# Seven half-block products in place of eight for the folded weight of an mLSTM and feed-forward kernel

## The chip, the cores and the metric

The kernel runs on one core of a Trainium2 chip. A core has TensorE (matrix products, results go to PSUM), VectorE and ScalarE (both read PSUM), GpSimd (works on SBUF alone) and queues that issue DMAs. PSUM has eight banks here; four belong to one pool of this kernel and are handed out again and again. The metric is the device time of one execution in microseconds (us).

## The reference, cut to what matters

An mLSTM cell over 768 tokens, for 4 batches of 8 heads of 40, gives `y`; its rows, 3072 tokens of 320, go through a multiplicative feed-forward block. There is no nonlinearity after the product of the two branches:

```python
x = attn_out.transpose(0, 2, 1, 3).reshape(B * S, H * D)   # 3072 x 320
a = x @ w1                                                # 320 x 1024
b = x @ w2                                                # 320 x 1024
h = a * b @ w3                                            # (a * b) @ w3, 1024 x 1024
out = h @ w_out                                           # 1024 x 320
```

So `w3` and `w_out` can be multiplied once: `w3o = w3 @ w_out`, 1024 x 320, the folded weight; then `out = (a * b) @ w3o`.

## The kernel before, in words

All of it is written out by a loop over `s`, called a step in this document. A step handles one block of 128 tokens of one batch in the cell (there are 24), and beside it a share of the feed-forward work of earlier blocks. The order of TensorE's instructions is the order in which they are written (`mm` and `transpose` chain each to the one before, L84 to L95); the other engines keep their own order too, in-order queues each, and an instruction waits there for what it reads and for the buffer that it writes.

In the steps that matter here, 9 to 16, TensorE does this, in order: the transposes of a finished block of `y` (`px`, L485); the products of the folded weight (`fold`, L253); two blocks of the feed-forward's first layer (`up`, tiles `pa`, `pb`, `pa`, `pb`, with their remainders `wr` in `up_rest`); and the cell's products (tiles `cell`). Every `px`, `wp`, `pa` and `pb` takes one bank of the pool of four (`mps`, L77). Their readers free them: `px` and `pa` are read by ScalarE, `pb` by VectorE (L639), `wp` by ScalarE (L264).

VectorE does in a step, in order: the two products L639 that finish the first layer's blocks; the cell's outputs and states, L423 to L445 (here `h` at L423 is the first that reads the step's own `cell` products); the transposes of the next `k` and `q` (L317); and two chunks of `w3` turned from their packed form to float32 and transposed (`convert`: L199, L200, L248). Sixteen such chunks, of half a row block each, are turned: one in step 7, three in step 8, two in each of steps 9 to 14 (`n_cvt`, L814).

GpSimd decays the states (L335: one decay that waits for nothing new, one that waits for VectorE's L404), weights `v` (L330), masks the weights of the next block (L308), and copies the last columns of `y` (L476), which the `px` transposes of the following step but one read.

The folded weight takes eight rounds, one for each 128 rows of `w3`: eight products of 128x128 by 128x320 each, summed in one bank, then one scaled copy by ScalarE:

```python
        for ki in range(FO):
            mm(wp, w3T[:, ki, :], wo[:, ki, :], start=(ki == 0), stop=(ki == FO - 1))
        nc.scalar.mul(out=w3o[:, ko, :], in_=wp, mul=UP ** -2)
```

A product in float32 appears in the trace as two matmul records, so the 64 products are 128 records. A row block's round runs in the step after the next one that follows its conversion: two in step 10, one in each of steps 11 to 16. In step 16 the second layer begins (`ffn_out`, tiles `po`), which reads `w3o`.

Of the kernel before, what the change touches and what calls it, by code (L numbers as in the profile page):

```python
# [8 lines left out]
FP = mybir.dt.float32  # L9
U32 = mybir.dt.uint32  # L10
AF = mybir.ActivationFunctionType
OP = mybir.AluOpType
UP = 2.0 ** 9
# [3 lines left out]
def kernel(  # L17
# [26 lines left out]
    nc = tc.nc  # L44
# [3 lines left out]
    P = 128  # L48
# [6 lines left out]
    DM = H * D  # L55
    BH = B * H
    DFF = moe_w1.shape[1]
    FO = DFF // P
# [6 lines left out]
    const = ctx.enter_context(tc.tile_pool(name="const", bufs=1))  # L65
    wst = ctx.enter_context(tc.tile_pool(name="wst", bufs=2))
# [10 lines left out]
    def mps(shape, name):  # L77
        pool = banks.pop(0)
        banks.append(pool)
        return pool.tile(shape, FP, name=name, tag="m")  # L80
# [3 lines left out]
    def in_order(ins):  # L84

        if last:
            tc.add_manual_dep(ins.ins, last.pop().name, mybir.DependencyInfo(
                mybir.DependencyClass.NoSync, mybir.DependencyReason.DATA), reason="in_order")
        last.append(ins.ins)

    def mm(out, lhsT, rhs, start=True, stop=True):
        in_order(nc.tensor.matmul(out, lhsT=lhsT, rhs=rhs, start=start, stop=stop))  # L92
# [75 lines left out]
    wo = const.tile([128, FO, DM], FP, name="wo")  # L168
# [3 lines left out]
    w3o = const.tile([128, FO, DM], FP, name="w3o")  # L172
    CW = 512
# [23 lines left out]
    def to_f32(dst, raw):  # L197
        bits, V = dst.bitcast(U32), nc.vector
        V.tensor_scalar(out=bits, in0=raw[:, :, 1], scalar1=3, scalar2=None, op0=OP.logical_shift_left)  # L199
        V.tensor_tensor(out=bits, in0=bits, in1=raw[:, :, 0], op=OP.add)  # L200
# [8 lines left out]
    pend, scaled = [], []  # L209
# [18 lines left out]


    w3T_t = {}  # L230
    turned_w3, ready_w3 = [], []

    def scale_next(early=False):
        scaled.append(pend.pop(0))
        scale(scaled[-1][1], early)

    def convert():
        if not scaled:
            scale_next()
        dst, raw, ko, half = scaled.pop(0)  # L240
        if dst is not None:
            to_f32(dst, raw)
            return
        w3 = wst.tile([128, CW], FP, name="w3", tag="w3")
        to_f32(w3, raw)
        if half == 0:
            w3T_t[ko] = wst.tile([128, FO, 128], FP, name="w3T", tag="w3T")
        nc.vector.transpose(out=w3T_t[ko].rearrange("c k (m r) -> c m k r", r=32)[:, 2 * half:2 * half + 2],  # L248
                            in_=w3.rearrange("r (m c k) -> r m k c", m=2, k=FO))
        if half:  # L250
            turned_w3.append(ko)

    def fold():  # L253
        while ready_w3:
            w3_mm(ready_w3.pop(0))
        ready_w3.extend(turned_w3)
        turned_w3.clear()

    def w3_mm(ko):
        w3T = w3T_t.pop(ko)  # L260
        wp = mps([128, DM], "wp")
        for ki in range(FO):
            mm(wp, w3T[:, ki, :], wo[:, ki, :], start=(ki == 0), stop=(ki == FO - 1))
        nc.scalar.mul(out=w3o[:, ko, :], in_=wp, mul=UP ** -2)  # L264


    qT_t, kT_t, vw_t, before_t, y_t, x_t = {}, {}, {}, {}, {}, {}
# [25 lines left out]
    def rows_of_u(n):  # L293
        c, b = divmod(n, B)
        nc.vector.transpose(out=weights_tile(n).rearrange("p h (t i) -> p h t i", t=2),
                            in_=UT[:, :, (0, 2, 1)[c], b * H:(b + 1) * H].rearrange("p t h -> p h t").unsqueeze(3).to_broadcast([P, H, 2, 32]))
# [171 lines left out]
    def x_turn(n):  # L468
        gr, j = divmod(n, GT)
        if j == 0:  # L470
            x_t[gr] = ffn.tile([128, KC, TG], FP, name="xT", tag="xT")
        nc.vector.transpose(out=x_t[gr][:, :, j * P:(j + 1) * P].rearrange("c k (m r) -> c k m r", r=32),
                            in_=back_t.pop(n).rearrange("r m k c -> r k m c"))
# [21 lines left out]
    f_sb, a, F, U, on = (gates[0:RG, i * TC:(i + 1) * TC] for i in range(5))  # L495
# [72 lines left out]
    for i, r in enumerate(third):  # L568
        V.tensor_tensor_scan(out=M[r, 1:GC + 1], data0=F3[r, :, L - 1], data1=U3[r, :, L - 1], initial=M[r, 0:1],
                             op0=OP.add, op1=OP.max)  # L570
# [24 lines left out]
    for i, r in enumerate(third):  # L595
        nc.gpsimd.tensor_tensor(out=pick[r, :, i, :], in0=pair[r].to_broadcast([BH, B * NP, GC]), op=OP.mult,
                        in1=dec[r].unsqueeze(1).to_broadcast([BH, B * NP, GC]))
# [11 lines left out]
    nc.scalar.activation(out=g, in_=U, func=AF.Exp)  # L609
    scale_next(True)  # L610
    convert()

    ffn = ctx.enter_context(tc.tile_pool(name="ffn", bufs=2))


    ab_t = {}
# [51 lines left out]
    def up_by_seven(gr, f, bank, aside_by):  # L668
# [61 lines left out]

        return single, shared, left, product

    def ffn_out(blocks, pos=None):

        pos = pos or [mps([P, DM], "po") for _ in blocks]
        for (gr, j), po in zip(blocks, pos):
            for f in range(FO):
                mm(po, ab_t[gr][j // 2][:, f, j % 2 * P:(j % 2 + 1) * P], w3o[:, f, :], start=(f == 0), stop=(f == FO - 1))
        for (gr, j), po in zip(blocks, pos):
            o_sb = ffn.tile([P, DM], FP, name="o_sb", tag="o_sb", bufs=2)  # L740
            nc.scalar.copy(out=o_sb, in_=po)  # L741
            t0 = j * S + gr * P
            nc.scalar.dma_start(out=out[t0:t0 + P, :], in_=o_sb)


    KH, NH = FO // 2, DM // 2

    def out_weight_sums():

        T_o.extend(m[:, i * KH * NH:(i + 1) * KH * NH].rearrange("p (f n) -> p f n", n=NH)  # L750
                   for m, i in ((v_all, 0), (gates, 0), (gates, 1), (q_all, 0)))
        (B11, B12), (B21, B22) = ([w3o[:, k * KH:(k + 1) * KH, i * NH:(i + 1) * NH] for i in range(2)] for k in range(2))
        T1, T2, T3, T4 = T_o
        for dst, p, q in ((T1, B12, B11), (T2, B22, T1), (T3, B22, B12), (T4, B21, T2)):
            yield nc.gpsimd.tensor_tensor(out=dst, in0=p, in1=q, op=OP.subtract)

    T_o, S_o = [], {}
    wsums = out_weight_sums()

    def quarters_of_ab(gr, j):  # L760
        return [[ab_t[gr][j][:, k * KH:(k + 1) * KH, t * P:(t + 1) * P] for k in range(2)] for t in range(2)]
# [1 line left out]
    def ab_sums(gr, j):  # L763
        mem = [t.rearrange("p h d -> p (h d)") if j == 0 else io.tile([P, H, L], FP, name="pw", tag="pw", bufs=5)
               .rearrange("p h t -> p (h t)") for t in kbuf]
        S1, S2, S3, S4 = S_o[gr, j] = [t.rearrange("p (f t) -> p f t", t=P) for t in mem]
        (A11, A12), (A21, A22) = quarters_of_ab(gr, j)
        for dst, p, q, op in ((S1, A21, A22, OP.add), (S2, S1, A11, OP.subtract), (S3, A11, A21, OP.subtract),
                              (S4, A12, S2, OP.subtract)):
            nc.vector.tensor_tensor(out=dst, in0=p, in1=q, op=op)  # L770

    def out_by_seven(gr, j, sums=None):
# [25 lines left out]
        for t in range(2):  # L798
# [3 lines left out]
    ups = [(gr, [f, f + 1], slice(j * 2 * P, (j + 1) * 2 * P)) for gr in range(3) for j in range(2)  # L802
           for f in range(0, FO, 2)]
    downs = [(gr, j) for gr in range(NG) for j in range(GT)][:14]
    outs = [(gr, j) for gr in range(3, NG) for j in range(2)][1:]
    summed = list(outs)
    sevens = [(gr, f) for gr in range(3, NG) for f in range(FH)]
# [5 lines left out]
    todo = w12[5:] + [("wo", i, 0) for i in range(FO)] + [("w3", ko, part) for ko in range(FO) for part in range(2)]  # L813
# [6 lines left out]
    for s in range(len(n_up)):  # L820
# [28 lines left out]
        while s >= N_DVE and turned < min(s - 2, NY):  # L849
            x_trans(turned)  # L850
            turned += 1
        fold()
        if s >= len(n_up) - 2:
            ab_sums(*summed.pop(0))
        def pairs():
# [62 lines left out]
        with tc.issue_after(gated.ins) if gated else nullcontext():  # L918
            if seven:
                seven[3]()  # L920
            for _ in range({NU: 1, NU + 1: 3}.get(s, 0)):
                next(wsums)
            if s == NU + 1:
                ab_sums(*summed.pop(0))
            if NY <= s - 2 < NU:
                x_turn(s - 2)
            for n in () if s == 1 else (s + 2,) if s < B else (s + 2, s + 3) if s == B else (s + 3,):
                if n < N_U:
                    rows_of_u(n)
            if N_DVE <= s + 1 < NU:  # L930
                gated = turn(s + 1)
            if s - 2 in range(4 * GT - 1, NU, GT):
                token_sums((s - 2) // GT)
            if s < len(n_up) - 2 and n_out[s + 1] and s > NU + 2:
                ab_sums(*summed.pop(0))
# [31 lines left out]
        with tc.issue_after(gated.ins) if N_DVE <= s + 1 < NU else nullcontext():  # L967
            for _ in range(n_cvt[s] if s < len(n_cvt) else 0):
                convert()
                converted += 1  # L970
        if s >= ahead:
            while pend and len(scaled) < 2:
                scale_next()
# [6 lines left out]
            for ins in keep_order(front):  # L980
                behind.enter_context(tc.issue_after(ins))
    behind.close()
    assert not ups and not sevens and not downs and not outs and not summed and not todo and not pend and not turned_w3 and not ready_w3, (len(ups), len(downs), len(todo), len(pend))
# [1 line left out]
_INS = ['q', 'k', 'v', 'i_gate', 'f_gate', 'o_gate', 'moe_w1', 'moe_w2', 'moe_w3', 'moe_w_out']  # L985
_OUTS = [((3072, 320), 'float32')]
# [25 lines left out]
```

## Time and profile before

| what | value |
|---|---|
| median of 3 runs | 426.35 us (425.69 to 426.39) |
| the profiled execution | 427.89 us, of which the program's span is 425.8 us |
| TensorE busy | 414.1 us, 97% |
| VectorE, ScalarE, GpSimd busy | 313.5, 150.1, 154.3 us |
| products of the folded weight (`wp`) | 128 records, 35.9 us, between 108.3 and 209.7 us |
| steps 9, 10, 11, 12, 13, 14, 15 by the start of `px` (step 9: of `pa`) | 96.6, 107.2, 127.7, 142.9, 158.9, 174.2, 189.5 us |

A busy share says how long an engine had something in it, not what sets the end. The profile's groups give counts and durations by line and tile; the timeline gives the order on one engine, with the idle time before an instruction and what ended it; the answer by windows gives busy time, the TensorE clock that was granted and DMA traffic in chosen stretches.

### The profile page before, as it was taken

Reading aid. Unit: us, or ns where it says so; the run is one execution under the profiler, and the core shown is the slowest. Engines: PE = TensorE matmul, PEld = TensorE weight load, DVE = VectorE, ACT = ScalarE, POOL = GpSimd, SP = SyncE. Lnnn points to the kernel's source line nnn. Section 1 sums busy time; section 2 is a strip of 40 time slices with the busy share of each in tenths; the row PEclk is TensorE's granted clock in tenths of the full one; section 3 lists DMA queues with packets and bytes.
Section 4 is the critical chain, followed back from the end, with each engine's and each line's share of the span. In section 5 each row is a group of like instructions: output and inputs, shape, how many; then the busy total and the mean of one; then the engine's idle time right before and its main releaser. Section 6 shows DMA issues by size and latency. Waiting matters only on the chain.

```text
span 425.8 us, 13079 instructions
## 1 busy us (share of the span) xinstructions
PE 414.1 (97%) x5353; PEld 335.3 (79%) x5353; DVE 313.5 (74%) x635; ACT 150.1 (35%) x404; POOL 154.3 (36%) x211
## 2 busy tenths in 40 slices
PE   7989989999999999999999999999999999999996
PEld 4768878888688788787777778788778879888896
DVE  6676986888949779778736966596868699575971
ACT  4766865567723623630433313032311110210000
POOL 4421342233303303303307751546453587542100
PEclk9989999999999999999999999999999999999999
DMA  8999998598977776985425675756421120000001
GB/s 186 204 173 245 214 144 140 134 193 180 215 183 154 166 182 135 181 164 105 89 80 130 153 141 121 142 133 117 87 44 36 35 39 2 31 2 31 2 32 62
DMA packets 135211, 51.15 MB, mean 120 GB/s; under 512 B 109360, under 2 KB 126960, under 8 KB 135152
## 3 DMA queue, kind: packets, MB, share of 16 engines
q1 hardware_dynamic: 131552, 46.29, 53.9%
q10 hardware_dynamic: 3600, 4.03, 2.7%
q8 instruction: 42, 0.69, 0.7%
q14 instruction: 17, 0.14, 0.1%
HBM read 44.50 MB, written 5.80 MB: 118 GB/s over the span
## 4 chain that ended last, share of the span: by engine, by line
PE 53%; issue 20%; DVE 7%; POOL 7%; SPq 7%; DMA 5%; ACT 1%; POOLq 0%; DVEq 0%
PE cell L92 17%; PE pa L92 12%; PE o L92 8%; PE pb L92 8%; PE p L92 3%; POOL pw L308 3%; SPq L184 3%; DVE w3T L666 2%; PE pt L95 1%; POOL vw L330 1%; SPq L148 1%; DMA raw<-in_moe_w_dram 1%; PE fill L92 1%; POOL raw L659 1%; POOL state L335 1%
## 5 line engine op out<-in xcount | busy, mean ns | idle before, releaser
L335 POOL TENSOR_TENSOR state<-state,decay 128x164 f32<-128x164 f32 x40 | 20.0, 500 | 154.8 <-DVE state L404 129.0
L92 PE MATMUL pa<-xT,w 128*128 128x256 f32 x240 | 60.4, 382 | 0.0
L92 PEld LDWEIGHTS pa<-xT,w 128*128 128x128 f32 x240 | 44.4, 190 | 6.8 <-DVE h L430 0.4
L303 ACT ACTIVATE pw<-pw,aT 128x64 f32<-128x64 f32 x184 | 46.4, 339 | 3.2 <-ACT o_sb L741 1.9
L92 PE MATMUL pb<-xT,w 128*128 128x256 f32 x192 | 45.4, 379 | 0.0
L729 POOL TENSOR_TENSOR ab<-ab,a_sb 128x512 f32<-128x512 f32 x22 | 29.4, 1356 | 32.2 <-DVE ab L684 32.2
L92 PEld LDWEIGHTS pb<-xT,w 128*128 128x128 f32 x192 | 36.4, 190 | 5.0
L711 POOL TENSOR_TENSOR wo<-wo 128x512 f32<-128x512 f32 x22 | 27.4, 1268 | 29.8 <-DVE wo L686 29.8
L92 PE MATMUL pa<-xT,wr 64*64 64x256 f32 x384 | 37.0, 386 | 0.5 <-DVE wr L200 0.5
L92 PE MATMUL wp<-wo,w3T 128*128 128x320 f32 x128 | 35.9, 433 | 1.1 <-DVE ab L639 0.6
L308 POOL TENSOR_SCALAR_AFFINE_SELECT pw<-pw 64x512 f32<-64x512 f32 x48 | 35.8, 746 | 3.0 <-ACT pw L303 1.2
L92 PE MATMUL pb<-xT,wr 64*64 64x256 f32 x384 | 36.4, 380 | 0.0
L92 PE MATMUL cell<-w3o,ab 128*128 128x320 f32 x128 | 35.4, 432 | 0.0
L638 ACT ACTIVATE a_sb<-pa 128x512 f32<-128x512 f32 x24 | 14.3, 598 | 59.0 <-PE pb L92 59.0
L639 DVE TENSOR_TENSOR ab<-pb,a_sb 128x512 f32<-128x512 f32 x24 | 16.4, 688 | 23.2 <-ACT a_sb L638 22.8
L92 PEld LDWEIGHTS wp<-wo,w3T 128*128 128x128 f32 x128 | 23.8, 190 | 10.5 <-DVE ab L639 0.8
L92 PEld LDWEIGHTS cell<-w3o,ab 128*128 128x128 f32 x128 | 24.3, 190 | 9.5
L92 PEld LDWEIGHTS pa<-xT,wr 64*64 64x64 f32 x384 | 18.9, 132 | 15.4 <-issue 8.8
L686 DVE SCALAR_TENSOR_TENSOR a_sb<-pa,wo 128x512 f32<-128x512 f32 x12 | 8.3, 689 | 29.8 <-PE pa L92 29.8
L430 DVE TENSOR_TENSOR h<-cell,h 64x164 f32<-64x164 f32 x88 | 28.6, 326 | 1.6
L92 PE MATMUL po<-w3o,ab 128*128 128x320 f32 x96 | 26.4, 433 | 0.0
L92 PEld LDWEIGHTS po<-w3o,ab 128*128 128x128 f32 x96 | 18.1, 190 | 7.3
(180 smaller groups left out, 846.4 us busy)
## 6 DMA issues: line engine op xcount, KB each, us to landing
raw<-in_moe_w_dram SPq DMA_DIRECT2D x64, 128.0 KB, 3.4
kbuf<-in_k_dram SPq DMA_DIRECT2D x24, 160.0 KB, 4.5
v_all<-in_v_dram SPq DMA_DIRECT2D x24, 160.0 KB, 4.9
o_in<-in_o_gate_dram SPq DMA_DIRECT2D x24, 160.0 KB, 4.8
pw<-U_d SPq DMA_DIRECT2D x28, 128.0 KB, 3.5
raw<-in_moe_w_dram SPq DMA_DIRECT2D x5, 512.0 KB, 6.7
raw<-in_moe_w_out_dram SPq DMA_DIRECT2D x8, 320.0 KB, 4.1
gates<-in_k_dram SPq DMA_DIRECT2D x28, 80.0 KB, 2.5
```

The source lines that it names most:

```text
L92: in_order(nc.tensor.matmul(out, lhsT=lhsT, rhs=rhs, start=start, stop=stop))
L184: nc.sync.dma_start(out=dst, in_=src)
L303: nc.scalar.activation(out=pw[:, h, :], in_=src[:, h, :], func=AF.Exp, bias=aT[:, c, b * H + h:b * H + h + 1])
L308: nc.gpsimd.affine_select(out=pw[r], in_=pw[r], compare_op=OP.is_ge, fill=0.0, base=0, pattern=[[0, H], [1, L]], channel_multiplier=-1)
L335: nc.gpsimd.tensor_tensor(out=new, in0=old, op=OP.mult, in1=decay[:, b * NP:(b + 1) * NP, 2 * c + x:2 * c + x + 1] .to_broadcast([P, NP, D1]))
L430: nc.vector.tensor_tensor(out=part, in0=ph[x][halves[e]], in1=part, op=OP.add)
L638: nc.scalar.mul(out=a_sb, in_=pa, mul=UP ** -2)
L639: nc.vector.tensor_tensor(out=ab_t[gr][j][:, fs[0]:fs[-1] + 1, t0:t0 + a_sb.shape[-1]], in0=pb, in1=a_sb, op=OP.mult)
L666: nc.vector.tensor_tensor(out=dst, in0=p, in1=q, op=OP.subtract)
L686: nc.vector.scalar_tensor_tensor(out=out, in0=p, scalar=UP ** -2, in1=q, op0=OP.mult, op1=OP.add)
L711: aside_by.tensor_tensor(out=kept[j][:, 1:4:2], in0=kept[j][:, 1:3], in1=kept[j][:, 3:4].to_broadcast([128, 2, TH]), op=OP.add)
L729: aside_by.tensor_tensor(out=t[:, f:FO:FH, :], in0=t[:, f:FO:FH, :], in1=a, op=OP.mult)
```

## The change: what it does, and the diff

The product of each 256 rows of `w3` with `w_out` is cut into halves in rows, in the summed dimension and in columns. In place of eight half-block products of 128x128 blocks by 160 columns, seven are made, from sums and differences of the halves (A for `w3`, B for `w_out`). Two of them need no sums (`fold_first`, in steps 9, 11, 13 and 15, one bank, copied by ScalarE); the other five are made a step later (`fold_second`, in steps 10, 12, 14 and 16, three banks, called `p67`, `p5` and `p34`), and VectorE adds them up in the place of the folded weight (the five adds).

The sums of the `w_out` halves, T1 to T4, are made once by GpSimd, two at the end of step 7 and two in step 8; the sums of the `w3` halves, S1 to S4, by GpSimd at the end of steps 8, 10, 12 and 14, in memory that is free then. In step 15 T4 moves, by one more GpSimd subtraction, since its place is part of the folded weight. The tile `w3` has one buffer in place of two, and the output tiles lie in the memory of T1.

```diff
-    def fold():
-        while ready_w3:
-            w3_mm(ready_w3.pop(0))
...
+    def fold_weight_sums():
...
+        for dst, p, q in ((T1, B12, B11), (T2, B22, T1), (B12, B22, B12), (T4, B21, T2)):
+            yield nc.gpsimd.tensor_tensor(out=dst, in0=p, in1=q, op=OP.subtract)
+
+    def fold_sums(i):
...
+        for dst, p, q, op in ((S1, A21, A22, OP.add), (S2, S1, A11, OP.subtract), (A21, A11, A21, OP.subtract),
+                              (S4, A12, S2, OP.subtract)):
+            nc.gpsimd.tensor_tensor(out=dst, in0=p, in1=q, op=op)
+
+    def fold_products(pairs):
+        wp = mps([128, len(pairs), NH], "wp")
+        for x, (a, b) in enumerate(pairs):
+            for k in range(KH):
+                mm(wp[:, x], a[:, k, :], b[:, k, :], start=(x == k == 0), stop=(x == len(pairs) - 1 and k == KH - 1))
+        return wp
...
+    def fold_first(i):
...
+        wp = fold_products(((A11, B11), (A12, B21)))
+        if i == FO // 2 - 1:
+            nc.gpsimd.tensor_tensor(out=B21, in0=B21, in1=fold_T[1], op=OP.subtract)
+            fold_T[3] = B21
+        nc.scalar.mul(out=fold_of(i)[:, 0:3:2], in_=wp, mul=UP ** -2)
+
+    def fold_second(i):
...
+        p67 = fold_products(((S2, T2), (S3, T3)))
+        p5 = fold_products(((S1, T1),))
+        p34 = fold_products(((S4, B22), (A22, T4)))
+
+        def add(out, p, c):
+            nc.vector.scalar_tensor_tensor(out=out, in0=p, scalar=UP ** -2, in1=c, op0=OP.mult, op1=OP.add)
+
+        add(C[:, 1], p67[:, 0], C[:, 0])
+        nc.vector.tensor_tensor(out=C[:, 0], in0=C[:, 0], in1=C[:, 2], op=OP.add)
+        add(C[:, 2], p67[:, 1], C[:, 1])
+        add(C[:, 1:4:2], p5.to_broadcast([128, 2, NH]), C[:, 1:3])
+        add(C[:, 1:3], p34, C[:, 1:3])
...
-        fold()
+        i, second = divmod(s - 9, 2)
+        if 0 <= i < FO // 2:
+            (fold_second if second else fold_first)(i)
...
+            for _ in range(2 if s == 8 else 0):
+                next(fsums)
...
+        for _ in range(2 if s == 7 else 0):
+            next(fsums)
+        if s in range(8, 16, 2):
+            fold_sums((s - 8) // 2)
```

## The prediction, made before the changed kernel ran

> **What bounds the kernel now.** I read the busy shares first, then the groups, then the timelines of TensorE and VectorE over two of the steps that change.
>
> ```profile
> PE 414.1 (97%) x5353; PEld 335.3 (79%) x5353; DVE 313.5 (74%) x635; ACT 150.1 (35%) x404; POOL 154.3 (36%) x211
> ...
> L92 PE MATMUL wp<-wo,w3T 128*128 128x320 f32 x128 | 35.9, 433 | 1.1 <-DVE ab L639 0.6
> ```
>
> TensorE is busy 97% of the span, and the folded weight takes 35.9 us of it. Fewer products would shorten the span one for one, if nothing else came in their way. So I look at what stands close behind TensorE. Timeline of TensorE, step 13:
>
> ```profile
> 158.94 0.55 PE L95 MATMUL px<-ident,y 128*128 128x128 f32 x3
> 159.32 4.47 PE L92 MATMUL wp<-wo,w3T 128*128 128x320 f32 x16
> 163.63 1.89 PE L92 MATMUL pa<-xT,w 128*128 128x256 f32 x8
> 165.35 1.89 PE L92 MATMUL pb<-xT,w 128*128 128x256 f32 x8
> ```
>
> The round of `wp` takes 163.63 - 159.32 = 4.31 us, 269 ns a record. VectorE at the same time:
>
> ```profile
> 158.58 0.49 DVE L423 TENSOR_TENSOR h<-cell,gT 128x328 f32<-128x328 f32 x1
> ...
> 161.24 0.32 DVE L404 TENSOR_TENSOR state<-cell,state 128x164 f32<-128x164 f32 x1
> ...
> 169.15 1.10 DVE L248 STREAM_TRANSPOSE w3T<-w 128x512 f32<-128x512 f32 x1
> 172.40 0.69 DVE L639 TENSOR_TENSOR ab<-pb,a_sb 128x512 f32<-128x512 f32 x1 [2.15 <-ACT a_sb L638]
> 173.87 0.49 DVE L423 TENSOR_TENSOR h<-cell,gT 128x328 f32<-128x328 f32 x1
> ```
>
> From `h` (L423) VectorE works without a break to 170.25, 11.67 us, and is free for only 2.15 us before it needs TensorE's next blocks. It runs nearly a whole step behind. I write T(s) for the start of L423 in step s: T(8) to T(16) are 94.55, 108.81, 127.31, 142.60, 158.58, 173.87, 189.16, 204.45, 219.41.
>
> **What the Trainium skill says.** SBUF — State Buffer, Who interferes with whom: a VectorE instruction with two SBUF inputs, or in a two-port mode, and a GpSimd instruction that reads SBUF block each other for a whole instruction. The trace agrees. A sum of two SBUF tiles (L666) takes 418 ns alone, but beside GpSimd's sums:
>
> ```profile
> 238.22 1.12 DVE L666 TENSOR_TENSOR w3T<-xT 128x256 f32<-128x256 f32 x1
> 239.38 1.38 DVE L666 TENSOR_TENSOR w3T<-xT,w3T 128x256 f32<-128x256 f32 x1
> 240.68 1.49 DVE L666 TENSOR_TENSOR w3T<-xT 128x256 f32<-128x256 f32 x1
> ```
>
> TensorE: Matmul & The Clock Gate, What's actually happening: after an idle window of about 3.4 us the clock is halved until a busy window has passed. The trace shows this once, by windows (PE busy first, granted clock after POOL):
>
> ```profile
> 20.00:23.41 3.41, 2.23 (x52) 1.75 (x52) 2.81 (x8) 2.38 (x8) 2.14 (x4) 1.00 1.22 165
> 23.41:26.83 3.42, 3.42 (x29) 1.92 (x31) 3.04 (x9) 2.78 (x6) 0.53 (x2) 0.50 0.96 146
> ```
>
> A thin window is followed by one of 3.42 us at half clock, which costs 1.7 us of work.
>
> Perfetto Trace Analysis, Optimization Strategy: the same gap again and again on the engine that should be full can mean too few SBUF or PSUM buffers. No such gap is in the trace before; I expect one after.
>
> **What the change removes.** 128 records of 320 columns become 224 of 160 (4 x 7 x 4 products, two records each). The final products have this shape; timeline of TensorE:
>
> ```profile
> 352.48 1.25 PE L92 MATMUL o<-v_all,pw 128*128 128x160 f32 x8
> 353.57 0.71 PE L92 MATMUL o<-gates,pw 128*128 128x160 f32 x4
> ```
>
> Eight in 1.09 us, 136 ns each; weight loads do not slow them. So 128 x 0.269 = 34.5 us becomes 224 x 0.136 = 30.4: 4.0 us saved. `fold_first` takes 2.17 us, `fold_second` 5.43. Four scaled copies by ScalarE (0.44 us) go too; ScalarE is 35% busy, so worth nothing.
>
> **What it adds, and where.**
>
> The adds. In VectorE's order as built, the five adds stand after the conversions of the step before, ahead of L639. Their banks: in steps 10, 12 and 14 four banks are taken by `px`, `p67`, `p5`, `p34`, and the first `pa` behind them waits, as built, for the third add, the last to read `p67`; `pb` waits for the fourth, the second `pa` for the fifth. Before, that `pa` waited only for ScalarE. VectorE reaches the adds at T(s-1) + 11.67. An add of 128x160 from PSUM is 324 ns (L794); the one between SBUF tiles 0.26 to 0.32 (half of L666's, or L794's; I take 0.3). Three end 0.95 later, with 0.1 for the semaphore: `pa` starts at T(s-1) + 12.7. From `pa` to the next T is 173.87 - 163.63 = 10.24, so such a step takes 22.95 against 15.29. All of TensorE's later work stands behind that `pa`, the cell's products included, and VectorE waits for those. The adds' own time (2.0 us for all five) would fit into the 2.15 us gap; it is their place that costs.
>
> Steps 11, 13, 15: 15.29 - 4.31 + 2.17 = 13.15. VectorE needs 11.67 and then L639, which starts 1.47 before T: 13.14. It just fits.
>
> Step 9. `fold_first` now stands at its start and needs the first row block of `w3`, turned only in step 8. By the timelines, TensorE starts `pa` at 96.62, while that transposition begins at 101.98 and lasts 1.14: 6.5 us of waiting. GpSimd's T sums come on top (1.55 us each; L755 has 128x640 at 1,545 to 1,995 ns). T1 and T2 meet the last three conversions of step 7, T3 and T4 meet L443 and L445 of step 8. By the L666 rows each such instruction waits about one GpSimd sum: I take 2.8 + 1.5 = 4.3 us, from 0 to 6. The block is then there at 107.4, and T(9) = 107.4 + 2.17 + 12.19 (108.81 - 96.62) = 121.8.
>
> The S sums. Four of 1.27 us (L659), 5.1 in all, wait for the last conversion, T(s) + 11.67 in steps 10, 12, 14, so end at T(s) + 16.8. Behind them on GpSimd stand a state decay (0.46) and the copy of `y` (0.24). L404 of the next step wants the decay at T + 2.66, that is T(s) + 15.8, and gets it at 17.3: VectorE is 1.5 late, and so are the adds of steps 12, 14 and 16. The copy comes at T(s) + 17.5, while the `px` of step s+2 wants it at about 13.7: nearly 4 us of TensorE, hidden under the wait for the adds in steps 12 and 14, open in step 16. `weighted` and the masks are needed a step later, so nothing for them.
>
> The clock. Each wait of 6 us or more holds a whole window: 1.7 us of lost work after the waits in steps 9, 10, 12, 14 (bounds 0 and 3.4).
>
> The single `w3` buffer costs nothing: two conversions overlap today by 0.1 us. The output tiles keep two buffers. No DMA is added or moved.
>
> **The sum.** T(9) = 121.8 + 1.7 = 123.5. T(10) = 123.5 + 22.95 + 1.7 = 148.2. T(11) = +13.15 = 161.3. T(12) = +22.95 + 1.5 + 1.7 = 187.5. T(13) = 200.6, T(14) = 226.8, T(15) = 239.9. In step 16 no conversions stand ahead of the adds, so VectorE is early; but `px` is held to T(15) + 4.35, then 0.17, 5.43, 8.6 for `po`, 1.2 to T: T(16) = 259.7, against 219.41, which is 40.3 later. From step 17 on nothing changes. Against the profiled 427.89 that gives 468.2; the median lies 1.5 below the profiled run: 466.6 us.
>
> **The rivals.**
> - The products' saving arrives whole: 426.35 - 4.0 = 422.3, faster. Its mechanism: the third add ends before TensorE has finished `p34` (T(s-1) + 6.4). It decides if VectorE reached the adds 6 us earlier than its order allows, before the conversions. For it: GpSimd and ScalarE have room, and five adds fit VectorE's gap. Against it: the order as built. 2%.
> - Even out: the waits are there but cost only what is saved, 426. Nothing in the profile makes four waits that small. 1%.
> - The bank waits alone, with no halved clock, no T sums in VectorE's way and a decay in time: T(9) +8.8, step 10 +4.5, steps 11, 13, 15 -6.4, step 12 +7.0, step 14 +7.7, step 16 +3: about 25, so 451. For it: L666 is the only pair seen, and the clock was halved only once. 15%.
> - The clock stays halved for two windows after each wait, and contention is at its upper bound: 466.6 + 7 + 2 = 475, up to 485. For it: a wait that is split in two (`px`, then the adds) can make two thin windows. 12%.
>
> **How the numbers follow.** The forecast has 70%: 466.6, its own range 456 to 476. The range 446 to 483 takes in most of the two slow rivals on either side of it and leaves out the fast ones and the ends, about 2 in 10. About 0.2% is what can be told from no change; faster 0.02, same 0.01, slower 0.97.
>
> **What would show it.** In the chain of waits: a `pa` product waiting for VectorE's adds three times, 6 to 8 us each, a wait of 9 us or more for the first `w3T` at step 9, and `px` waiting for GpSimd's copy. In the windows: a clock below 1.00 between 97 and 260 us. Step lengths near 13 and 25 us in turn. `wp` at 224 records of some 30 us. The prediction is wrong if the adds find VectorE free early, if the first `w3T` is ready by the end of step 8, or if the rest after step 16 changes its length.

## The result, and the profile after

| kernel | median, us | lowest to highest | ratio, 95% interval |
|---|---|---|---|
| before | 426.02 | 424.24 to 426.39 | 1 |
| after | 467.94 | 467.29 to 468.38 | 1.0992, 1.0957 to 1.1026 |

The profiled execution of the changed kernel took 467.29 us, of which 465.6 are the program's span. Forecast were 466.6 for the median and 468.2 for the profiled execution.

The lines of the changed kernel's page that answer to those of before: busy shares, the granted clock by slices of 11.6 us (tenths of full speed), and one of the groups of `wp`.

```profile
PE 422.5 (91%) x5449; PEld 352.4 (76%) x5449; DVE 327.9 (70%) x655; ACT 147.8 (32%) x400; POOL 183.7 (39%) x232
...
PEclk9999999978979879979979999999999999999999
...
L92 PE MATMUL wp<-wo,w3T 128*128 128x160 f32 x104 | 20.6, 361 | 9.9 <-DVE w3T L247 9.9
```

TensorE is no longer full, and its clock dips in the slices from 93 to 244 us, where the change is. The waits of TensorE in the same kernel (total, how often, longest):

```profile
PE px L95 <- POOL y L533: 10.9, 3, 3.9
PE pa L92 <- DVE w3o L313: 10.1, 3, 6.5
PE wp L92 <- DVE w3T L247: 9.9, 1, 9.9
```

These are the three kinds of wait that the prediction named, 30.9 us in all. TensorE is busy 8.4 us longer (422.5 against 414.1) though its products are 4.0 shorter, so some 12.4 us are work stretched by the halved clock; 30.9 + 12.4 - 4.0 is 39.3 of the 39.8 us by which the span grew. The windows agree: from 95 to 260 us the clock is halved for 41.0 us, TensorE is busy for 25.9 of them, and half of that is 13.0. Timeline of TensorE in step 10 after the change (start, duration):

```profile
119.68 0.55 PE L95 MATMUL px<-ident,y 128*128 128x128 f32 x3
...
124.41 1.25 PE L92 MATMUL wp<-w3o,w3T 128*128 128x160 f32 x8
132.17 3.75 PE L92 MATMUL pa<-xT,w 128*128 128x256 f32 x8 [6.51 <-DVE w3o L313]
135.72 2.00 PE L92 MATMUL pb<-xT,w 128*128 128x256 f32 x8
```

TensorE has finished all five products at 125.7 and stands still for 6.5 us. When `pa` starts, eight records take 3.75 us in place of 1.89. VectorE in the same step:

```profile
119.33 0.49 DVE L480 TENSOR_TENSOR h<-cell,gT 128x328 f32<-128x328 f32 x1
...
130.01 1.09 DVE L247 STREAM_TRANSPOSE w3T<-w 128x512 f32<-128x512 f32 x1
131.03 0.28 DVE L313 SCALAR_TENSOR_TENSOR w3o<-wp,w3o 128x160 f32<-128x160 f32 x1
131.34 0.32 DVE L316 TENSOR_TENSOR w3o<-w3o 128x160 f32<-128x160 f32 x1
131.70 1.52 DVE L313 SCALAR_TENSOR_TENSOR w3o<-wp,w3o 128x160 f32<-128x160 f32 x3
```

The adds begin 11.7 us after `h`, when the last conversion is done, and `pa` begins 12.84 after `h`. The products have been ready since 6.3 after `h`. The adds themselves are short.

The steps, by the start of `h` (L423 before, L480 after):

| step | before | forecast | after |
|---|---|---|---|
| 9 | 14.26 | 28.95 | 24.76 |
| 10 | 18.50 | 24.7 | 25.02 |
| 11 | 15.29 | 13.15 | 13.16 |
| 12 | 15.98 | 26.2 | 26.67 |
| 13 | 15.29 | 13.15 | 13.74 |
| 14 | 15.29 | 26.2 | 24.43 |
| 15 | 15.29 | 13.15 | 13.16 |
| 16 | 14.96 | 19.75 | 22.55 |

From step 11 on the odd steps gain what the shorter products promise. The others lose far more.

### The profile page after: what moved, and what is told of

It reads as the page before. It is cut to its first block, busy times and chain, and to the rows that moved or that the text cites. A ratio compares the mean times of both kernels' runs of the same rounds, so it can differ in the third digit from the quotient of the medians.

```text
span 465.6 us, 13323 instructions
## 1 busy us (share of the span) xinstructions
PE 422.5 (91%) x5449; PEld 352.4 (76%) x5449; DVE 327.9 (70%) x655; ACT 147.8 (32%) x400; POOL 183.7 (39%) x232
## 4 chain that ended last, share of the span: by engine, by line
PE 56%; DVE 12%; SPq 11%; issue 10%; DMA 4%; POOL 4%; ACT 1%; DVEq 0%; POOLq 0%; ACTq 0%
PE cell L92 16%; PE pa L92 16%; PE pb L92 10%; PE o L92 7%; SPq L139 4%; PE p L92 4%; DVE w3T L247 2%; SPq L184 2%; DVE w L200 2%; SPq L153 2%; DMA raw<-in_moe_w_dram 2%; DMA q_all<-in_k_dram 1%; SPq L159 1%; DVE w3T L723 1%; DVE w L199 1%
## 5 line engine op out<-in xcount | busy, mean ns | idle before, releaser
L92 PE MATMUL pa<-xT,w 128*128 128x256 f32 x240 | 62.9, 394 | 10.1 <-DVE w3o L313 10.1
L92 PE MATMUL pb<-xT,w 128*128 128x256 f32 x192 | 47.0, 388 | 0.9 <-DVE w L200 0.9
L696 DVE TENSOR_TENSOR ab<-pb,a_sb 128x512 f32<-128x512 f32 x24 | 16.3, 684 | 39.2 <-ACT a_sb L695 38.8
L92 PEld LDWEIGHTS pb<-xT,w 128*128 128x128 f32 x192 | 37.7, 197 | 6.8 <-DVE w L200 1.3
L92 PE MATMUL wp<-wo,w3T 128*128 128x160 f32 x104 | 20.6, 361 | 9.9 <-DVE w3T L247 9.9
L92 PEld LDWEIGHTS wp<-wo,w3T 128*128 128x128 f32 x104 | 19.4, 243 | 10.1 <-issue 10.1
```

Source lines behind the costliest of these rows:

```text
L696: nc.vector.tensor_tensor(out=ab_t[gr][j][:, fs[0]:fs[-1] + 1, t0:t0 + a_sb.shape[-1]], in0=pb, in1=a_sb, op=OP.mult)
```

## The experiments

All of them start from the changed kernel, except where another is named. The kernel before, run beside each group of them, had a median of 425.8 to 426.5 us.

**Take the banks off VectorE.** ScalarE copies the three banks of products out of PSUM, into memory of the S sums that is free by then, and the adds read the copies.

```diff
-        p67 = fold_products(((S2, T2), (S3, T3)))
-        p5 = fold_products(((S1, T1),))
-        p34 = fold_products(((S4, B22), (A22, T4)))
+        for to, pairs in ((fold_p[i][0][:, 0:2], ((S2, T2), (S3, T3))), (fold_p[i][0][:, 2:3], ((S1, T1),)),
+                          (fold_p[i][1], ((S4, B22), (A22, T4)))):
+            nc.scalar.copy(out=to, in_=fold_products(pairs))
+            kept.append(to)
```

> ScalarE copies p67, p5 and p34 out of PSUM at once, and VectorE adds from those copies; all else is as in the changed kernel. My theory, that the banks wait for VectorE's late adds: the first pa of step 10 starts about 6.3 us after L480 in place of 12.8 (6.5 us less, and 1.7 of halved clock less); in steps 12 and 14 the wait of px for GpSimd's copy stays, so only 2.1 and 1.5 us fall away, and about 1 of clock; about 456 us in all. Rival, that the adds cost by their own time and by contention on VectorE, whose work is as long as before: within 2 us of the changed kernel, 466 to 470.

Measured: 451.05 us (449.88 to 452.94), 16.9 less than after. The wait for the adds is gone from the trace, and the other two stand as they were (`px` 10.1, `wp` 9.9). Step 10 fell from 25.02 to 16.91. More was won than expected (456 us): steps 12 and 14 became 4.5 and 5.4 us shorter, where 2.1 and 1.5 of waiting and about 1 of clock were forecast. The clock is halved for less time, 20.5 us in place of 41, and in step 14 not at all.

**Move the S sums behind the decay and the copy of `y`,** to the start of the next step on GpSimd.

```diff
-        if s in range(8, 16, 2):
-            fold_sums((s - 8) // 2)
...
+        if s in range(9, 17, 2):
+            fold_sums((s - 9) // 2)
         if NY <= s - 2 < NU:
             get_back(s - 2)
```

> The S sums are written a step later, behind the state decay and the copy of y on GpSimd. My theory: the three waits of px for GpSimd (10.9 us in the trace) vanish, but in steps 12 and 14 the wait for the adds behind them grows by nearly as much; only VectorE's earlier start (1.4 and 0.9 us) and all of step 16 (some 5 us with its halved clock) are won: about 460 us. Rival, that the waits add up: 10.9 us and the halved clock around them, about 453 us.

Measured: 466.57 us (464.67 to 467.19), 1.4 less than after: neither number. The waits of TensorE in this kernel:

```profile
PE pa L92 <- DVE w3o L313: 20.6, 3, 7.4
PE wp L92 <- DVE w3T L247: 9.9, 1, 9.9
PE po L92 <- DVE w3o L313: 1.2, 1, 1.2
```

The wait for `y` has gone, and the wait for the adds has doubled: in steps 12 and 14 the first had stood in the shade of the second. Of the steps that had waited for `y` only step 16, with no conversions ahead of the adds, became shorter (18.56 in place of 22.55). Steps 12 and 14 became 0.6 and 2.5 longer: in step 14 the one long wait keeps the clock halved for 10.24 us, where it had been 6.83.

**Make the first two products of the first 256 rows at the start of step 10,** behind `px`, in place of step 9.

```diff
-        if 0 <= i < FO // 2:
+        if s == 10:
+            fold_first(0)
+        if 0 <= i < FO // 2 and s > 9:
             (fold_second if second else fold_first)(i)
```

> The first two products of the first 256 rows stand at the start of step 10 in place of step 9. My theory: the wait of 9.9 us for the first turned block of w3 vanishes, with the halved clock behind it; L480 of step 9 comes at about 111 us (108.8 before, and 2.2 for the T sums) in place of 119.3, and the 2.2 us of products hide under the wait of step 10: about 459.6 us. Rival, that VectorE is late in step 9 anyway and the wait only moves: 465 us or more.

Measured: 460.71 us (455.39 to 462.75), 7.2 less than after; with this spread the gain is rough. The wait of 9.9 us is gone and T(9) is 111.3 in place of 119.3. A wait of 4.4 us for VectorE's L696 is new in step 10: VectorE had come late out of step 9.

**All three.** No further edit.

> The three edits together: ScalarE reads the banks, the S sums stand behind the copy of y, the first products stand in step 10. My theory, that the waits for the adds and for GpSimd's copy cover each other, so that only both edits together free TensorE: steps 10 to 16 take 18.6, 13.2, 16.4, 13.2, 16.4, 13.2, 16.1 us from L480 to L480, and the time is about 424.5 us, the 4.0 us of products less what the T sums (2.2 us) cost. Rival, that the three gains only add: about 440 us.

Measured: 435.03 us (432.51 to 435.93), ratio 1.0189, 1.0139 to 1.0239. That is 32.9 less than after, while the three alone give 16.9, 1.4 and 7.2, 25.5 in all: two waits in one step cover each other, so the second remedy pays only beside the first. By steps: step 12 takes 26.67 us in the changed kernel, 22.17 with the first remedy, 27.29 with the second and 17.50 with all three. The time that the theory named, 424.5, was missed by 10.5 us. Against the kernel before, steps 8, 9 and 16 are 1.7, 2.3 and 3.6 us longer (the first two beside the T sums), and step 10, forecast at 18.6, holds the 4.4 us for VectorE and takes 18.88. The profiled execution, the fastest of the four at 432.51, leaves some 2.5 us of the median without an account.

**The place of the adds or their number?** The five products and the adds are written ahead of the conversions of the step before. With that the products also come ahead of their step's `px` in TensorE's order; before, they stood behind it.

```diff
+        if s in (9, 11, 13, 15):
+            fold_second((s - 9) // 2)
         with tc.issue_after(gated.ins) if N_DVE <= s + 1 < NU else nullcontext():
             for _ in range(n_cvt[s] if s < len(n_cvt) else 0):
                 convert()
```

> The five adds of steps 10, 12, 14 and 16, and nothing else, stand on VectorE ahead of the conversions of the step before; memory, sums, products and banks stay as in the changed kernel. Theory (the place of the adds costs, not their number): the wait of TensorE for the adds, 3 times, ends at about T(s-1) + 8.6 in place of 12.8, so step 10 is 4 to 6 us shorter and steps 12, 14 up to as much; in step 16 the adds come earlier too. The wait for GpSimd's copy of y (px, 3.9 us in each of three steps) stays and covers part of it. About 450, from 446 to 456. Rival (five more VectorE instructions a step are too many whatever their place; the conversions then come late in their stead): 464 to 468.

Measured: 448.98 us (447.43 to 449.48), ratio 1.0522. VectorE does the same instructions in step 10, now in this order:

```profile
125.09 1.08 DVE L374 STREAM_TRANSPOSE qT<-gates 128x512 f32<-128x512 f32 x1
126.02 0.30 DVE L313 SCALAR_TENSOR_TENSOR w3o<-wp,w3o 128x160 f32<-128x160 f32 x1
126.36 0.33 DVE L316 TENSOR_TENSOR w3o<-w3o 128x160 f32<-128x160 f32 x1
126.72 1.51 DVE L313 SCALAR_TENSOR_TENSOR w3o<-wp,w3o 128x160 f32<-128x160 f32 x3
128.15 0.42 DVE L199 TENSOR_SCALAR w<-raw 128x512 uint32<-128x512 uint32 x1
```

TensorE in the same step:

```profile
123.92 1.25 PE L92 MATMUL wp<-w3o,w3T 128*128 128x160 f32 x8
125.00 0.49 PE L95 MATMUL px<-ident,y 128*128 128x128 f32 x3
127.19 1.97 PE L92 MATMUL pa<-xT,w 128*128 128x256 f32 x8 [1.69 <-DVE w3o L313]
```

The adds begin 6.9 us after `h` (119.12) and not 11.7, and TensorE waits for them 1.69 us in place of 6.51. Step 10, in which `px` waits for nothing in either kernel, fell from 25.02 to 18.39 us: that is what their place costs there, with their number unchanged. Steps 12 and 14 fell by 6.2 and 5.3 us, but there a second thing changed: `px`, now behind the products, no longer waits for the copy of `y`. It had waited 10.9 us in all in steps 12, 14 and 16, and the expectation had this wait stay. The 19 us of the whole are the work of both moves, and only step 10 separates them.

**What does the clock cost?** To the kernel with the S sums moved, nine products of the identity are added behind `p34`, into the bank of `px`. Nobody reads them.

```diff
+        for _ in range(9 if i < FO // 2 - 1 else 0):
+            mm(last_px[0], ident, ident.unsqueeze(1).to_broadcast([P, KF + 1, P]))
```

> The kernel with the sums one step later (466.6), in which TensorE waits three times for the adds, 20.6 us in all; in each of these three waits, behind the products of p34, nine products of the identity, which nobody reads, are written into the bank of px. They compute nothing that is wanted and take some 5.8 us of a wait of 7. Theory (the waits cost twice: themselves, and then work at half clock): the clock is not halved after steps 10, 12 and 14, and each of these steps takes about 23 us in place of 25.5, 27.3 and 26.9: about 456, from 453 to 460. Rival (the clock costs nothing beside the waits): 466 to 468, or slower where the extra products end behind the adds.

Measured: 457.91 us (457.37 to 458.11), 8.7 less for more work. Timeline of TensorE in step 10 with the filling:

```profile
126.35 6.07 PE L92 MATMUL px<-ident 128*128 128x384 f32 x18 [0.23 <-ACT xT L547]
132.57 1.99 PE L92 MATMUL pa<-xT,w 128*128 128x256 f32 x8
```

`pa` starts at the same distance from `h` as before (12.8 us after 119.8; 12.9 without the filling) and runs at full clock, 1.99 us in place of 3.75. After 110.3 us the clock is not halved again. From `pa` to the next `h` the steps 10, 12 and 14 took 12.64, 13.16 and 13.09 us without the filling and 10.35 each with it. So each of these three waits of about 7 us cost 2.3 to 2.8 us more than its own length by the timelines, 2.9 by the medians.

**Place the sums where VectorE reads PSUM.** From the kernel with all three remedies: T1 stands behind the conversions of step 6, T2 and T3 behind those of step 7, T4 behind the first S sums; `p5` goes ahead of `p67`; T4 stays where it is until the last adds.

```diff
+        for x in range({7: 1, 8: 2, 9: 1}.get(s, 0)):
+            summed_T = next(fsums)
+            if x == 0:
+                tc.add_manual_dep(summed_T.ins, conv_last[0].name, mybir.DependencyInfo(
...
-            nc.gpsimd.tensor_tensor(out=B21, in0=B21, in1=fold_T[1], op=OP.subtract)
-            fold_T[3] = B21
-        nc.scalar.mul(out=fold_of(i)[:, 0:3:2], in_=wp, mul=UP ** -2)
+        nc.scalar.mul(out=fold_p[i][3] if i == FO // 2 - 1 else fold_of(i)[:, 0:3:2], in_=wp, mul=UP ** -2)
```

> The kernel with all three remedies (435.0) and four more: T1 at the end of step 6's conversions, T2 and T3 at the end of step 7's, T4 behind the S sums at the start of step 9, each where VectorE reads PSUM; p5 (which needs S1 alone) ahead of p67; T4 stays where it is until the last adds, so that the one subtraction of step 15 goes; the first two products of the last 256 rows are kept apart by ScalarE until then. Theory: step 8 is 1.7 us shorter (11.9 in place of 13.5), step 9 2.1 (14.4), step 10 1.4 (17.5), steps 12 and 14 together 0.7, step 16 2.4 (16.1): 8.3 us in all, 426.7; where all of it comes and the clock is never halved, 424, which is less than before. Rival (VectorE stays the bound in these steps, whatever GpSimd does): 430 to 435.

Measured: 430.16 us (427.12 to 433.2), ratio 1.0083, 1.0051 to 1.0114. The number lies in the rival's range, but its reason does not hold: step 8 fell from 13.54 to 11.86, which is its length before the change, and step 9 from 16.52 to 14.86. What was missed is step 10. It grew from 18.88 to 20.85, where 17.5 was forecast, by a wait that was not expected:

```profile
PE wp L92 <- ACT xT L549: 3.1, 1, 3.1
```

With five tiles on four banks in step 10, `p34` takes the bank of `px`. ScalarE's copy out of it stood behind scalings of raw weights that waited for their transfer.

**Three further edits, one on top of the other.** The scaling ahead starts one step later; the last five adds stand ahead of the transpositions of `k` and `q`; one conversion moves from step 8 to step 5.

```diff
-    pinned, ahead = 32, 9
+    pinned, ahead = 32, 10
...
+            if s == 15:
+                x_trans(turned)
+                turned += 1
+                fold_second(3)
             if N_DVE <= s + 1 < NU:
                 gated = turn(s + 1)
...
-    n_cvt = [0, 0, 2, 0, 1, 2, 3, 3, 3] + [2] * 6
+    n_cvt = [0, 0, 2, 0, 1, 3, 3, 3, 2] + [2] * 6
```

> The kernel with its sums placed (430.2) and one more edit: the scaling of two raw chunks ahead begins in step 10 in place of step 9, so that ScalarE's copy of px in step 10 does not stand behind two scalings that wait for their data (TensorE waits 3.1 us there for the bank of px). Theory: step 10 is 17.8 us in place of 20.9, and nothing else moves: 427.0, from 425 to 429. Rival (the two scalings are missed in step 10 and VectorE waits for them there): 429 to 432.

> The kernel before it in this list, and in step 16 the last five adds ahead of the two transpositions of k and q on VectorE, so that the first product of the second layer that reads the last 256 rows does not wait for them (0.8 us now). Theory: step 16 is 16.6 us in place of 17.4: 0.8 us less than the kernel before it, 426.2. Rival (the transpositions are then late for the cell of step 17): no less than the kernel before it.

> The kernel before it in this list, and one conversion of weights fewer in step 8 and one more in step 5, so that VectorE is not the bound of step 9 (14.86 us now, 14.26 in the kernel before the change). Theory: 0.6 us less than the kernel before it, 425.6, below the 426.5 of the kernel before the change. Rival (step 5 is bound by VectorE or by the weights' transfer): as much as or more than the kernel before it in this list.

Measured: 426.57 us (ratio 1.0013, 0.9992 to 1.0033), 424.84 (0.997, 0.9948 to 0.9991) and 423.24 (0.9942, 0.9926 to 0.9958). Each did what it was meant to: step 10 fell to 17.60, step 16 to 16.11, and with the third edit steps 8 to 10 take 43.17 us together in place of 44.71. The second and the third gave 1.7 and 1.6 us by the medians, where 0.8 and 0.6 were forecast; the steps show 1.05 and 1.5. All that TensorE waits for in steps 8 to 16 of the last kernel:

```profile
PE cell L92 <- issue: 1.2, 1, 1.2
PE pt L95 <- issue: 0.7, 1, 0.7
```

No wait for an engine is left.

**Is it the seven products that make the last kernel faster?** Its last edit could serve the eight products too. So it was made alone in the kernel before the change, and the last kernel was run once more beside it.

> The kernel before the change, with eight products, and one edit alone: one conversion of weights fewer in step 8 and one more in step 5, which the last kernel had beside its seven products. Theory (the seven products give what their shorter time promises, and this edit at most the waits of TensorE behind step 8's conversions, 0.6 us and 0.5 us in the profile of before): 424.7 to 425.8. Rival (this edit is what made the last kernel faster, and the seven products nothing): 423.2.

> The last kernel of the study once more, beside the kernel before with the same edit: seven products, all remedies. Theory: 423.2 again, so 1.5 to 2.5 us below the eight products with the edit. Rival: no less than them.

Measured: 426.21 us for eight products with the edit, ratio 1.0006 (0.9977 to 1.0035), and 424.24 for seven, ratio 0.9954 (0.9933 to 0.9975). The edit gives nothing that can be told to the kernel before. From T(7) to T(16) the profiles show 137.1 us for eight products with it and 133.4 for seven, 3.7 less, near the 4.0 that the prediction worked out for the products; the medians show 2.0 here and 2.5 in the runs before. The later scaling could serve the eight products too and was not tried there. But between 76 and 216 us TensorE waits only 1.4 us in all in the kernel before, less than the 2.0 and 2.5 by which the medians differ. So the saving exists, and this kernel is faster than the kernel before by about half a per cent, and faster than the changed one.

## Why the prediction was right, point by point

**The products.** Forecast 2.17 us for `fold_first`, hence 13.15 us for an odd step. Measured 13.16 in steps 11 and 15, and eight records of 160 columns 1.09 us apart. Right. (Step 13 was 0.6 longer, by a pause of TensorE of 0.57 us for which the profile names no cause.)

**The adds' place.** Forecast `pa` at T(s-1) + 12.7, measured + 12.84 in step 10; with VectorE's 1.5 on top + 14.2 in steps 12 and 14, measured + 14.66 and + 14.11. The five adds took 2.2 us (forecast 2.0). That the place costs and not the number was argued then; it is shown by step 10 of the experiment that moved the adds (6.6 us). One reading was loose: VectorE does not work "without a break" over the 11.67 us, it waits 0.47 of them for GpSimd's decay. The sum does not change by it.

**Step 9.** The mechanism was right: a wait of 9.9 us for the first `w3T`. Two terms were too large. The sum of 107.4 for the block had 4.3 us for the T sums; the first block was ready at 105.0. And 12.19 us from `pa` to T(9) held a stretch in which VectorE, not TensorE, had been late before; from `pa`, now at 109.1, to T(9) it is 10.25. Together 4.3 us, which covers T(9)'s error of 4.2 (119.3 for 123.5). VectorE in step 9 after the change:

```profile
98.38 1.58 DVE L500 SCALAR_TENSOR_TENSOR o_in<-o_in,den 128x320 f32<-128x320 f32 x1
99.99 1.73 DVE L502 TENSOR_TENSOR y<-h,o_in 128x320 f32<-128x320 f32 x1
```

Before the change these two take 0.76 and 0.49 us. They run beside T3 and T4 (98.05 to 101.37), and are longer by 0.8 and 1.2 us: the trace agrees with the Trainium skill (SBUF — State Buffer, Who interferes with whom), by which a VectorE instruction with two SBUF inputs and a GpSimd instruction that reads SBUF block each other. The conversions of step 7 lost 1.68 us to T1 and T2 (step 8: 13.54 in place of 11.86). T(8) hides this: the profile of before holds a pause of TensorE of 1.5 us before T(6), and the profile after does not. The block itself ends at 104.97, 1.85 us later than before, at the same T(8). So the T sums cost 1.68 and 1.85, 3.5 us, not much less than the 4.3 of the sum; most of the 2.4 us by which it came early is this pause, which the forecast had taken over.

**The S sums.** The copy of `y` came as late as forecast: `px` was held in steps 12, 14 and 16, 10.9 us in all (forecast: nearly 4 each), hidden in the first two and open in the third. The experiment that moved these sums alone shows it: of the three only step 16 gained. VectorE reached the adds 1.8 us late in step 12 and 1.3 in step 14 (forecast 1.5).

**The clock.** Forecast 1.7 us after each of four waits. By windows (us; busy time of PE, PEld, DVE, ACT, POOL; granted clock; DMA) in the changed kernel:

```profile
95.00:98.41 3.41, 0.21 (x2) 0.00 (x0) 2.83 (x12) 3.41 (x12) 0.78 (x2) 1.00 0.78 205
98.41:101.82 3.41, 0.00 (x0) 0.00 (x0) 3.38 (x4) 3.06 (x6) 3.41 (x3) 0.50 1.30 191
101.82:105.24 3.42, 0.13 (x1) 0.16 (x1) 3.16 (x4) 0.00 (x0) 2.47 (x4) 0.50 0.59 136
105.24:108.65 3.41, 3.41 (x13) 3.41 (x14) 3.01 (x5) 0.00 (x0) 0.00 (x0) 0.50 0.70 215
```

An idle window is followed here by halved ones, until one has been full. In steps 12, 14 and 16 the same follows a window with 1.5 to 2.1 us of waiting in it. Only the work of TensorE that falls into halved windows is stretched, and it counts only where nothing behind it waits longer. In step 9 the products took 3.97 us for 2.17, and from `pa` to T the steps 10 and 12 took 12.18 and 12.01 for 10.24: 1.8, 1.9 and 1.8 us, so there the price was right. In step 14 it was not due: the halved stretch, from 200.8 to 207.6, lies ahead of `pa`, under the wait for the adds, and from `pa` to T it is 10.32. And step 16 was given none, since only waits of 6 us or more were thought to hold a whole window, and it has one: its `px` wait, 3.76 us, halves the clock from 238.3 to 245.2, and the step took 22.55 us where 19.75 were forecast. This is the one step of the sum that failed by omission.

**How near the number came.** T(16) was forecast at 259.7 and came at 258.05. Step 9 was 4.2 us shorter than forecast and step 14 1.7, step 16 was 2.8 longer and steps 10, 12 and 13 together 1.5. That these nearly cancel is luck; the waits, their order and their causes were not.

**The end.** From T(16) to the end of the span 207.5 us against 206.4: step 20 took 19.38 us for 18.45, with another such pause of TensorE at 299.7. "From step 17 on nothing changes" was therefore a little off. The step from the profiled run to the median, minus 1.5, was taken over from the kernel before and failed: the median after lies 0.65 above the profiled run. The forecast for the profiled run itself was 0.9 too high.

**The rivals.** "The bank waits alone" at 451 falls with the windows above and with the filled waits. "Two windows after each wait" saw rightly that the clock stays halved for more than one window (10.24 us around the wait in step 9), but most of such a stretch lies under the wait itself. The split wait that it names did make two halved stretches, in step 12 (159.8 to 166.7 and 173.5 to 176.9), but the first lies under the wait for the adds. "The saving arrives whole" was right about the saving and wrong about this kernel: it needs the adds' banks free, the sums placed and step 10's banks free in time. What makes the pauses called "issue", and why they sit in other places from one kernel to the next, was not tried; the last section says what the traces show of them.

## What to carry to other kernels

Ask of every added reader of a PSUM bank what stands ahead of it in its engine's queue, not how long it takes: 2 us of adds behind 5 us of conversions made one step 6.6 us longer here, and copying the banks out by an idle engine, or writing the products and adds ahead, gave 17 to 19 of the 42 us back. Where two waits fall in one step, remove both before judging either. The seven products paid here only when their sums lay beside work that they do not disturb and the banks came free in time; in such a case look for the 4 us that were promised, and try the last edits on the old kernel too.

## What was not expected of the hardware

A GpSimd sum of 128x512, 1.27 us, holds up a VectorE instruction of 8 elements to a partition about as long as the large ones above. VectorE beside an S sum, in the kernel with the sums placed:

```profile
107.35 1.34 DVE L493 TENSOR_TENSOR h<-cell,h 64x164 f32<-64x164 f32 x4
108.73 1.00 DVE L501 TENSOR_SCALAR den<-h 128x8 uint32<-128x8 uint32 x1
```

and the same two in the kernel before:

```profile
109.33 1.34 DVE L430 TENSOR_TENSOR h<-cell,h 64x164 f32<-64x164 f32 x4
110.71 0.17 DVE L438 TENSOR_SCALAR den<-h 128x8 uint32<-128x8 uint32 x1
```

The four that read PSUM are not touched; the tiny one takes 1.00 us in place of 0.17. And TensorE shows pauses that the profile puts down to nothing ("issue"): of those from 0.5 us up, 1.5 and 0.5 in the profile of before, and 0.7 to 1.2, 3.9 us in all, four times in that of the fastest kernel. The traces hold a lead: in all fourteen profiles together there are 27 such pauses, and each begins 1.0 to 2.2 us after a packet of DMA queue 8, which the page calls "instruction", has started; these packets come 10.2 us apart on average. This points to the fetching of instructions, but no run tests it. The pauses are as large as the differences between the last three kernels, which is why these were told apart by medians and not by their profiles.
